# Attention over a recurrent state with a squared-ReLU feed-forward: the state of batches 3 to 7 loaded after the last quarter of w_out, and a list schedule with longer assumed loads

## The chip, the cores and the metric

One Trainium2 chip, one core of it. The metric is device time in microseconds (us), lower is better: the median of the timed executions. One further execution was profiled; all durations in this document come from profiled executions. Engines are named as the profile names them: PE is the matmul engine, PEld its weight loads, DVE, ACT and POOL the three engines that copy, activate and do general work, SP the engine that only issues transfers. A transfer is issued by POOL, SP or ACT and moved by 16 DMA engines that all of them share.

## What is computed

Eight batches, 8 heads, 512 tokens, a state of 32 rows a head, 64 columns; the feed-forward is 512 to 2048 to 512.

```python
def _attn_ref(x, state):                       # x (8,8,512,64), state (8,8,32,64)
    scores = (1/8) * x @ state^T               # softmax over the 32 state rows
    xread = softmax(scores) @ state            # 512 rows a head
    scores2 = (1/8) * state @ x^T              # softmax over the 512 tokens
    sread = softmax(scores2) @ x               # 32 rows a head
    return concat([xread, sread], axis=2)
def _moe_ref(x, w_in, w_out, s, b):            # x: heads side by side, 8*544 rows of 512
    r = maximum(x @ w_in, 0)
    return (s * (r * r) + b) @ w_out
```

## The kernel before

**What is multiplied.** For the 512 token rows of a batch the kernel doesn't form `xread`: it multiplies the state by w_in once per batch (tiles `Mps`, copied to `M`), and multiplies that by the normalised attention weights `a4`, which gives the feed-forward's hidden rows `h` in 16 pieces `f` of 128 rows. `h` is cut at zero by ACT (sometimes DVE) into `g`, squared by DVE, and multiplied by w_out into the two output banks `o_0` and `o_1`. Batch 0 does the last product plainly (`rows_mm`); batches 1 to 7 use a seven-product scheme that needs sums of blocks of `g` (`pd`, DVE) and of w_out (`u`, DVE). The state rows (`V`, `sr`, `srdT`, `h_sr`, `g_sr`) are collected over all batches and go through the feed-forward last.

**Loads.** w_in is loaded in four column pieces `wi_0` to `wi_3`, w_out in four row pieces `wo_0` to `wo_3`, x in a tile `xn_b` a batch; these are issued by POOL (lines 353, 363, 374), which converts to 16 bits on the way, and run one behind the other in its queue. The state comes in three pieces in 32 bits: `stf` for batch 0 (ACT's queue), `stf1` for 1 and 2, `stf2` for 3 to 7 (128 partitions of 640 numbers, 320 KB). `late` (line 381) issues the last two: POOL writes zeros into the tile (line 383), which takes it to POOL's place in the program, and SP issues the transfer behind that (line 384). `stf2` is converted by POOL into `st16` (`cast_st`, line 300), and one transposing transfer on SP (`dma_stT`, line 429) makes `stTd`, the transposed state of batches 3 to 7. `Mps` and the scores `T` of batch 3 are the first to read `stTd`. Batches 3 to 7 also get their transposed x, `xT`, by transposing transfers on SP (line 445), and every batch gets `aT` so (line 604, from `a2`, DVE), which `V` reads. SP issues in program order: `stf2`, the two `aT` pairs of batches 0 and 1, `stTd`, then the four `xT` pieces of batch 3.

**What sets the order.** Every step is handed to `Plan.add` with an engine, an assumed duration, a priority key (lower goes first) and names that it needs and makes. `Plan.order` then plays the program through with these assumed durations and writes each engine's instructions in the order in which it would have started them. On the chip each engine runs its list strictly in that order and waits where something isn't there. Loads have an assumed pace: `("load", span)` lands `span` behind the load before it. `("tp", span)` is for other transfers: they land `span` after issue, or later while loads are still assumed to run. `K` (line 271) holds the constants that the keys are made of.

**The places around the change.** `seq` (line 390) is the list of loads. PE's matmuls all have line 197, through the helper `mm`. A PE step is named below by its output: `h_b_f` is piece f of batch b, `Mps_b_c` is the product with `wi_c`, `wsum_ps` the column sums of w_out for the bias, which need all four `wo`. `Mps_0_3` is the first reader of `wi_3`. Only two buffers hold `h` (pool `psH`), so an `h` starts when ACT or DVE has read the one two before it.

Of the kernel before, what the change touches and what calls it, by code (L numbers as in the profile page):

```python
# [13 lines left out]
class Plan:  # L14
# [6 lines left out]
    def add(self, eng, key, fn, needs=(), makes=(), bufs=(), land=None, tiled=False, after=0.0, spare=0.0):  # L21
        engs = dict([eng]) if isinstance(eng[0], str) else dict(eng)
        for p, b in bufs:
            self.pool_of[b] = p
            self.users[b] = self.users.get(b, 0) + 1
        self.ops.append((engs, key, fn, tuple(needs), tuple(makes), [b for _, b in bufs], land, tiled, after, spare))

    def order(self, filler, fill_until, ready):
# [21 lines left out]
        mode, channel, log, now, done_n = False, 7.0, [], 0.0, 0  # L50
# [17 lines left out]
        while done_n < len(ops):  # L68
            for e in free_at:
                if free_at[e] > now + 1e-9:  # L70
                    continue
                best = None
                look = self.look if e in ("ACT", "DVE") else 0.06
                for i in cand[e]:
                    if since[i] > now + look:
                        continue
                    t = soon(i) - now
                    if t > look:
                        continue
                    k = ops[i][1] + 20.0 * max(0.0, t)  # L80
                    if e == "PE" and ops[i][7] and mode:
                        k -= 4.0
                    if len(ops[i][0]) > 1 and e == "DVE":
                        k += ops[i][9]
                        if free_at["ACT"] <= now + 0.3:
                            continue
                    if best is None or k < best[0]:
                        best = (k, i, t)
                if best is not None and best[2] > 1e-9:
                    continue  # L90
                if best is None:
                    fill = 0.43 if now < 7.0 else 0.22
                    if e == "PE" and now < fill_until and not any(since[i] < now + fill for i in cand[e]):
                        free_at[e] = now + fill
                        times.append(free_at[e])
                        log.append((now, len(log), "PE", filler, "warm", free_at[e]))
                    continue
                i = best[1]
                engs, key, fn, needs, makes, bufs, land, tiled, after, spare = ops[i]
                for x in engs:  # L100
                    cand[x].discard(i)
                for b in bufs:
                    if b not in placed:
                        placed.add(b)
                        allocs[self.pool_of[b]].append(b)
                dur = engs[e]
                if e == "PE":
                    dur += 0.1 * (tiled != mode)
                    mode = tiled
                end = done = now + dur  # L110
                if land is not None:
                    kind, span = land
                    if kind == "load":
                        done = max(channel, end + 2.0) + span
                        channel = max(channel, done)
                    elif now < channel - 4.0:
                        end, done = now + 4.0, now + 9.0
                    else:
                        done = end + span
                free_at[e] = end  # L120
                times.append(end)
                times.append(done + self.hop)
                for m in makes:
                    ready[m] = done + self.hop
                for m in makes:
                    for j in waits.pop(m, ()):
                        count[j] -= 1
# [12 lines left out]
            now = min(nxt) if nxt else now  # L140
# [4 lines left out]
def kernel(  # L145
# [13 lines left out]
    nc = tc.nc  # L159
# [3 lines left out]
    B, H, S, D = x.shape  # L163
# [6 lines left out]
    NG = H // 4  # L170
# [47 lines left out]
    st_v = state.rearrange("b (g hf) j d -> (hf j) (b g) d", g=NG)  # L218
    NB_HW = 3
    stf = konst.tile([P, NG, D], FP32, name="stf")  # L220
    stf1 = konst.tile([P, (NB_HW - 1) * NG, D], FP32, name="stf1")
    stf2 = konst.tile([P, (B - NB_HW) * NG, D], FP32, name="stf2")
# [42 lines left out]
    def late_dma(dst, src):  # L265
# [3 lines left out]
        nc.sync.dma_start(dst, src)  # L269

    K = dict(
        h1=4.0, hs=0.6, M0=-5.6, M1=-0.7, T1=-1.2, x2=24.7, T2=23.1, D2=27.7, M2=23.7, V0=27.1, V1=25.0, u=12.2,
        us=2.0, pd1=12.5, o0=9.0, o2=22.8, w=25.2, r=-0.5, T=-14.5, D=3.1, Mb=5.6, V=12.0, S=3.6, S0=0.1,
        E=-4.5, L=-4.6, a4=-4.7, Mc=4.3, pd=3.5, sp=-0.2,
    )
    A = {b: {"E": {}, "a4": {}} for b in range(B)}
    G, PD, U, SN, OSB = {}, {}, {}, {}, {}
    stTd = konst.tile([P, (B - NB_HW) * NG, P], FP16, name="stTd")
    wi, wo = {}, {}
# [29 lines left out]
    add = plan.add  # L309
# [37 lines left out]
    def load(key, dur, span, fn, makes, bufs=(), after=0.0):  # L347
        add(("POOL", dur), key, fn, [], makes, bufs, ("load", span), after=after)

    def load_wi(c):  # L350
        def fn(e):
            wi[c] = wpool.tile([P, NKM, FC], FP16, name=f"wi_{c}")
            nc.gpsimd.dma_start(  # L353
                out=wi[c],
                in_=moe_w_in.rearrange("(k p) f -> p k f", p=P)[:, :, c * FC : (c + 1) * FC],
            )

        return fn

    def load_wo(q):  # L360
        def fn(e):
            wo[q] = wpool.tile([P, NKF // 4, DM], FP16, name=f"wo_{q}")
            nc.gpsimd.dma_start(  # L363
                out=wo[q],
                in_=moe_w_out.rearrange("(q f p) n -> q p f n", p=P, q=4)[q],
            )

        return fn

    def load_x(b, h0=0, h1=H):  # L370
        def fn(e):
            if h0 == 0:
                xn[b] = xpool.tile([P, H, SCH, D], FP16, name=f"xn_{b}", tag="xn")
            nc.gpsimd.dma_start(  # L374
                out=xn[b][:, h0:h1].rearrange("p h c d -> p h (c d)"),
                in_=x[b, h0:h1].rearrange("h (q c) d -> q h (c d)", q=P),
            )

        return fn

    def late(dst, src):
        def fn(e):
            nc.gpsimd.memset(dst, 0.0)
            nc.sync.dma_start(dst, src)

        return fn
# [1 line left out]
    gate = konst.tile([P, 2], FP16, name="gate")  # L388
    nc.gpsimd.tensor_copy(gate, ident16[:, 0:2])
    seq = [("wi", 0), ("x", 1), ("wi", 1), ("stf1",), ("wo", 0), ("wi", 2), ("wo", 1), ("wi", 3)]  # L390
    seq += [("wo", 2), ("wo", 3), ("x", 2), ("sb",), ("stf2",), ("x", 3), ("x", 4), ("x", 5)]
    for n, it in enumerate(seq):
        key = -40 + n
        if it[0] == "wi":
            load(key, 0.8, 4.2 if it[1] == 0 else 2.65, load_wi(it[1]), [it], after=3.4)
        elif it[0] == "wo":
            load(key, 0.8, 2.65, load_wo(it[1]), [it], after=3.4)
        elif it[0] == "x":
            b = it[1]
            load(  # L400
                key, 0.9, 2.8 if b == 1 else 3.8, load_x(b),
                [("x", b, i) for i in range(4)], [("xn", f"x{b}")], after=3.4,
            )
        elif it[0] == "stf1":
            load(key, 0.3, -3.0, late(stf1, st_v[:, NG : NB_HW * NG, :]), [it], after=3.4)
        elif it[0] == "stf2":
            load(key, 0.6, 1.0, late(stf2, st_v[:, NB_HW * NG :, :]), [it], after=3.4)
        else:
            load(key, 0.15, 0.1, late(s_bc, moe_s.to_broadcast((P, 1))), [("s",)], after=3.4)
            load(key + 0.1, 0.15, 0.1, late(b_bc, moe_b.to_broadcast((P, 1))), [("b",)], after=3.4)  # L410
    n1 = (NB_HW - 1) * NG
    add(
        DV(0.4), 0, lambda e: cast_st(e, stf1, NG, n1),
# [6 lines left out]
    for k in range(8):  # L420
        b, i = 6 + k // 4, k % 4
# [94 lines left out]
    def E_exp(b, g):  # L516
        def fn(e):
# [4 lines left out]
            for m in range(2):  # L522
                nc.scalar.activation(  # L523
                    a["E"][g][:, 256 * m : 256 * m + 256],
                    a["T"][m][:, g, :],
# [609 lines left out]
```

## Time and profile before

| | |
|---|---|
| median of 8 runs | 223.97 us (222.48 to 226.24) |
| the profiled execution's own time | 224.34 us |
| span of its instructions | 222.3 us |
| PE busy | 207.3 us, 93% |
| DVE busy | 164.5 us, 74% |
| ACT busy | 134.6 us, 61% |
| POOL busy | 37.5 us, 17% |
| moved by DMA | 24.04 MB |

The span runs from the first instruction of the program to its last; the profiled execution's time has about 2 us around it. Times inside the span are given as us from its start. In a timeline row stand start, duration, engine, line, operation, output<-input, shape and count; in square brackets the idle time of the engine before it and what ended it. Rows of consecutive instructions of one kind are merged, so a merged row's duration is from the first start to the last end. Matmuls are pipelined: what one costs in a row of equals is best read from the chain, where a row gives the time until the next kind begins. PEclk is the clock that PE was granted, 1.00 at full speed. An issue row gives KB and the us from issue to landing, a median where several are counted.

### The profile page before, as it was taken

Reading aid. Unit: us, or ns where it says so; the run is one execution under the profiler, and the core shown is the slowest. Engines: PE = TensorE matmul, PEld = TensorE weight load, DVE = VectorE, ACT = ScalarE, POOL = GpSimd, SP = SyncE. Lnnn points to the kernel's source line nnn. Section 1 sums busy time; section 2 is a strip of 40 time slices with the busy share of each in tenths; the row PEclk is TensorE's granted clock in tenths of the full one; section 3 lists DMA queues with packets and bytes.
Section 4 is the critical chain, followed back from the end, with each engine's and each line's share of the span. In section 5 each row is a group of like instructions: output and inputs, shape, how many; then the busy total and the mean of one; then the engine's idle time right before and its main releaser. Section 6 shows DMA issues by size and latency. Waiting matters only on the chain.

```text
span 222.3 us, 4924 instructions
## 1 busy us (share of the span) xinstructions
PE 207.3 (93%) x1967; PEld 132.0 (59%) x1967; DVE 164.5 (74%) x390; ACT 134.6 (61%) x293; POOL 37.5 (17%) x60
## 2 busy tenths in 40 slices
PE   5998759999999999999999999999999999999960
PEld 1443213543466767677766676667667777888650
DVE  1379447999898788877997799798889878754330
ACT  4669827779568565974997488559855544332100
POOL 4933111002034152102110101111112102100000
PEclk9999958999999999999999999999999999999997
DMA  6999999997059999902531212122202111210221
GB/s 200 188 200 154 192 201 198 197 172 174 0 134 170 132 167 228 140 10 94 118 99 30 99 47 76 29 97 72 71 18 86 49 47 53 97 47 19 78 80 62
DMA packets 41282, 24.04 MB, mean 108 GB/s; under 512 B 25772, under 2 KB 39340, under 8 KB 41260
## 3 DMA queue, kind: packets, MB, share of 16 engines
q0 software_dynamic: 13840, 15.21, 35.5%
q1 hardware_dynamic: 26860, 8.40, 22.3%
q8 instruction: 15, 0.25, 0.4%
q10 hardware_dynamic: 560, 0.13, 0.3%
q14 instruction: 7, 0.06, 0.1%
HBM read 17.37 MB, written 8.91 MB: 118 GB/s over the span
## 4 chain that ended last, share of the span: by engine, by line
PE 83%; DMA 11%; POOL 2%; DVE 0%; issue 0%
PE o L197 48%; PE h L197 23%; DMA wi<-in_moe_w_in_dram 10%; PE Mps L197 4%; PE h_sr L197 3%; PE V L197 1%; PE D L197 1%; DMA ident<-ident_const 1%; POOL wi L353 1%; PE T L197 1%; POOL wo L363 1%; PE wsum_ps L197 0%; PE bias_ps L197 0%; POOL xn L374 0%; PE xTps L197 0%; DVE osb_last L1075 0%
## 5 line engine op out<-in xcount | busy, mean ns | idle before, releaser
L756 ACT ACTIVATE g<-h 128x512 f16<-128x512 f32 x127 | 74.8, 606 | 50.6 <-PE h L197 48.7
L197 PE MATMUL h<-a,M 128*128 128x512 f16 x256 | 75.3, 385 | 0.3 <-ACT g L756 0.3
L762 DVE TENSOR_TENSOR g<-g 128x512 f16<-128x512 f16 x128 | 52.4, 422 | 6.7 <-ACT g L756 6.6
L197 PEld LDWEIGHTS <-pd 128*128 128x128 f16 x448 | 43.0, 98 | 17.9 <-issue 1.9
L197 PE MATMUL o<-wo,g 128*128 128x256 f16 (+1 forms) x288 | 52.6, 300 | 0.0
L197 PEld LDWEIGHTS <-g 128*128 128x128 f16 x400 | 38.9, 98 | 23.0 <-issue 2.6
L197 PE MATMUL o<-u,pd 128*128 128x256 f16 x336 | 50.5, 273 | 0.0
L998 POOL DMA_DIRECT2D out_dram<-c x24 | 16.3, 678 | 104.6 <-DVE c L990 87.5
L197 PEld LDWEIGHTS <-M 128*128 128x128 f16 x256 | 24.5, 99 | 12.9 <-issue 5.3
L990 DVE SCALAR_TENSOR_TENSOR c<-o,s_bc,bias_bc 128x512 f32<-128x512 f32 x28 | 21.0, 752 | 14.9 <-PE o L197 14.8
L298 ACT CAST M<-Mps 128x512 f16<-128x512 f32 x49 | 27.7, 606 | 1.0 <-PE Mps L197 1.0
L990 DVE SCALAR_TENSOR_TENSOR c<-o,s_bc,c 128x512 f32<-128x512 f32 x21 | 15.8, 750 | 9.0 <-PE o L197 8.8
L197 PE MATMUL o<-u,g 128*128 128x256 f16 x112 | 21.4, 273 | 0.0
L197 PE MATMUL o<-wo,pd 128*128 128x256 f16 x112 | 21.4, 273 | 0.0
L774 DVE TENSOR_TENSOR pd<-g 128x1024 f16<-128x1024 f16 x28 | 19.2, 686 | 0.3
L756 ACT ACTIVATE g_sr<-h_sr 128x256 f16<-128x256 f32 x16 | 6.1, 383 | 12.9 <-PE h_sr L197 12.9
L523 ACT ACTIVATE E<-T 128x256 f16<-128x256 f32 x32 | 11.9, 384 | 1.3 <-PE T L197 1.2
L374 POOL DMA_DIRECT2D xn<-in_x_dram x13 | 10.4, 820 | 10.0 <-DMA wi<-in_moe_w_in_dram 4.7
L785 DVE TENSOR_TENSOR pd<-g,pd 128x512 f16<-128x512 f16 x28 | 11.7, 419 | 0.1
L783 DVE TENSOR_TENSOR pd<-g,pd 128x512 f16<-128x512 f16 x28 | 11.7, 418 | 0.0
L300 DVE CAST M<-Mps 128x512 f16<-128x512 f32 x15 | 10.2, 685 | 0.6 <-PE Mps L197 0.6
L542 ACT ACTIVATE D<-D 128x512 f32<-128x512 f32 x16 | 8.7, 584 | 3.2 <-PE D L197 3.1
(62 smaller groups left out, 156.8 us busy)
## 6 DMA issues: line engine op xcount, KB each, us to landing
out_dram<-c POOLq DMA_DIRECT2D x24, 256.0 KB, 2.5
xn<-in_x_dram POOLq DMA_DIRECT2D x5, 512.0 KB, 24.4
wi<-in_moe_w_in_dram POOLq DMA_DIRECT2D x4, 512.0 KB, 14.0
wo<-in_moe_w_out_dram POOLq DMA_DIRECT2D x4, 512.0 KB, 21.9
xf<-in_x_dram SPq DMA_DIRECT2D x4, 256.0 KB, 3.3
out_dram<-osb POOLq DMA_DIRECT2D x4, 256.0 KB, 3.4
xn<-in_x_dram POOLq DMA_DIRECT2D x8, 128.0 KB, 5.8
out_dram<-c SPq DMA_DIRECT2D x4, 256.0 KB, 2.5
```

Source lines behind the costliest of these rows:

```text
L197: return nc.tensor.matmul(out, lhsT, rhs, start=start, stop=stop, tile_position=tp, is_transpose=is_transpose, skip_group_check=True,)
L298: nc.scalar.copy(dst, src)
L300: ENG[e].tensor_copy(dst, src)
L374: nc.gpsimd.dma_start(out=xn[b][:, h0:h1].rearrange("p h c d -> p h (c d)"), in_=x[b, h0:h1].rearrange("h (q c) d -> q h (c d)", q=P),)
L523: nc.scalar.activation(a["E"][g][:, 256 * m : 256 * m + 256], a["T"][m][:, g, :], AF.Exp, scale=scale, accum_out=a["rs"][:, g, m : m + 1],)
L756: nc.scalar.activation(g_of(name, f), OSB["h", name, f], AF.Relu)
L762: ENG[e].tensor_mul(g_of(name, f), g_of(name, f), g_of(name, f))
L774: nc.vector.tensor_tensor(pd[:, :, 0:2], g4[:, :, 1:2, :].to_broadcast((P, 2, 2, hS)), g4[:, :, 0:4:3, :], ALU.subtract,)
L783: nc.vector.tensor_tensor(pd[:, :, 2], g4[:, :, 3], pd[:, :, 0], ALU.subtract)
L785: nc.vector.tensor_tensor(pd[:, :, 3], g4[:, :, 2], pd[:, :, 2], ALU.subtract)
L990: nc.vector.scalar_tensor_tensor(t, src, s_bc, add, ALU.mult, ALU.add)
L998: ENG[e].dma_start(dst[:, rows:SCH:2, hD * h : hD * h + hD], SN[b, name])
```

## The change

`stf2` leaves the list of loads. It is issued by a step of its own, `load_stf2`: POOL copies two columns of `wo_3` into `stf2`, which can't happen before `wo_3` has landed, and SP issues the transfer behind that. The plan assumes that it lands 4 us after POOL's step (`"side"`, which no longer takes the delay of `"tp"` while loads run). The assumed spans of the loads grow (w_in and w_out 2.65 to 2.8, x 2.8 to 2.9 and 3.8 to 3.9), and 16 of the constants in `K` change, among them M1, T1, V1, D2, V, us. No computation changes, and the instructions are the same but for POOL's zeroing of `stf2`, which becomes the two-column copy, and the engine that runs some casts and cuts.

```diff
-                    elif now < channel - 4.0:
+                    elif kind == "tp" and now < channel - 4.0:
                         end, done = now + 4.0, now + 9.0
                     else:
                         done = end + span
...
-        h1=4.0, hs=0.6, M0=-5.6, M1=-0.7, T1=-1.2, x2=24.7, T2=23.1, D2=27.7, M2=23.7, V0=27.1, V1=25.0, u=12.2,
+        h1=4.3, hs=0.6, M0=-5.6, M1=0.9, T1=0.9, x2=24.4, T2=23.7, D2=25.5, M2=24.1, V0=27.6, V1=20.5, u=12.2,
...
-    seq += [("wo", 2), ("wo", 3), ("x", 2), ("sb",), ("stf2",), ("x", 3), ("x", 4), ("x", 5)]
+    seq += [("wo", 2), ("wo", 3), ("x", 2), ("sb",), ("x", 3), ("x", 4), ("x", 5)]
...
-            load(key, 0.8, 2.65, load_wo(it[1]), [it], after=3.4)
+            load(key, 0.8, 2.8, load_wo(it[1]), [it], after=3.4)
...
-        elif it[0] == "stf2":
-            load(key, 0.6, 1.0, late(stf2, st_v[:, NB_HW * NG :, :]), [it], after=3.4)
...
+    def load_stf2(e):
+        nc.gpsimd.tensor_copy(stf2[:, 0, 0:2], wo[3][:, 0, 0:2])
+        nc.sync.dma_start(stf2, st_v[:, NB_HW * NG :, :])
+
+    add(("POOL", 0.3), -21, load_stf2, [("wo", 3)], [("stf2",)], (), ("side", 4.0))
```

On POOL, behind the load of x for batch 2, stand before:

```order
L374 DMA xn_2_228<-in_x_dram 128x8x256
L383 MEMSET s_bc_114 128x1
L383 MEMSET b_bc_115 128x1
L383 MEMSET stf2_99 128x640
L374 DMA xn_3_262<-in_x_dram 128x8x256
L374 DMA xn_4_268<-in_x_dram 128x8x256
L374 DMA xn_5_287<-in_x_dram 128x8x256
L300 CAST st16_118<-stf2_99 128x10x64 x2
```

and now:

```order
L374 DMA xn_2_228<-in_x_dram 128x8x256
L383 MEMSET s_bc_114 128x1
L383 MEMSET b_bc_115 128x1
L374 DMA xn_3_255<-in_x_dram 128x8x256
L374 DMA xn_4_263<-in_x_dram 128x8x256
L374 DMA xn_5_273<-in_x_dram 128x8x256
L411 CAST stf2_99<-wo_3_217 128x2
L300 CAST st16_118<-stf2_99 128x10x64 x2
```

POOL's step that lets SP issue `stf2` has moved behind all loads up to x of batch 5, and now reads `wo_3`. SP's own list has kept its order.

On PE, from the second matmul of `h_1_4` on, stand before:

```order
L197 MATMUL h_1_4_473<-a4_1_1_413,M_1_325 128x512
L197 LDWEIGHTS stT_0_161
L197 MATMUL Mps_0_3_0_479<-wi_3_195,stT_0_161 32x512
L197 LDWEIGHTS stT_0_161
L197 MATMUL Mps_0_3_1_480<-wi_3_195,stT_0_161 32x512
```

and now the same `Mps_0_3` stands behind two `h`, four matmuls of `o_0` with `wo_1`, and two more `h`, of which these are the last:

```order
L197 MATMUL o_0_121<-wo_1_190,g_0_1_390 128x512
L197 LDWEIGHTS M_1_343
L197 MATMUL h_1_7_496<-a4_1_0_403,M_1_343 128x512
L197 LDWEIGHTS M_1_343
L197 MATMUL h_1_7_496<-a4_1_1_409,M_1_343 128x512
L197 LDWEIGHTS M_0_250
L197 MATMUL h_0_8_501<-a4_0_0_232,M_0_250 128x512
L197 LDWEIGHTS M_0_250
L197 MATMUL h_0_8_501<-a4_0_1_260,M_0_250 128x512
L197 LDWEIGHTS stT_0_161
L197 MATMUL Mps_0_3_0_505<-wi_3_195,stT_0_161 32x512
```

So `h_1_5`, `h_1_6`, `o_0` with `wo_1`, `h_1_7` and `h_0_8`, which stood right behind `Mps_0_3`, now stand right before it. On ACT the cuts of `h_1_5` and `h_1_6` now stand ahead of both casts of `Mps_1_2`, and the cut of `h_0_8` has gone to DVE. What follows on PE up to `wsum_ps` is the same work in nearly the same order. Further on, `T_3` stands about 0.7 us of PE's work earlier (`h_2_7` and three pairs of `o` have moved behind it, one `Mps` of batch 3 ahead of it), and `V` of batches 3 to 7 about 3 us earlier.

More of the change, by code (lines that the diff above doesn't have):

```diff
@@ L271 @@
     K = dict(
-        h1=4.0, hs=0.6, M0=-5.6, M1=-0.7, T1=-1.2, x2=24.7, T2=23.1, D2=27.7, M2=23.7, V0=27.1, V1=25.0, u=12.2,
-        us=2.0, pd1=12.5, o0=9.0, o2=22.8, w=25.2, r=-0.5, T=-14.5, D=3.1, Mb=5.6, V=12.0, S=3.6, S0=0.1,
-        E=-4.5, L=-4.6, a4=-4.7, Mc=4.3, pd=3.5, sp=-0.2,
+        h1=4.3, hs=0.6, M0=-5.6, M1=0.9, T1=0.9, x2=24.4, T2=23.7, D2=25.5, M2=24.1, V0=27.6, V1=20.5, u=12.2,
+        us=5.1, pd1=12.5, o0=9.6, o2=23.0, w=26.2, r=0.7, T=-14.8, D=3.1, Mb=5.5, V=8.6, S=3.6, S0=0.1, E=-4.5,
+        L=-4.6, a4=-4.7, Mc=4.3, pd=3.5, sp=-1.7,
     )
@@ L394 @@
         if it[0] == "wi":
-            load(key, 0.8, 4.2 if it[1] == 0 else 2.65, load_wi(it[1]), [it], after=3.4)
+            load(key, 0.8, 4.2 if it[1] == 0 else 2.8, load_wi(it[1]), [it], after=3.4)
         elif it[0] == "wo":
-            load(key, 0.8, 2.65, load_wo(it[1]), [it], after=3.4)
+            load(key, 0.8, 2.8, load_wo(it[1]), [it], after=3.4)
         elif it[0] == "x":
@@ L400 @@
             load(
-                key, 0.9, 2.8 if b == 1 else 3.8, load_x(b),
+                key, 0.9, 2.9 if b == 1 else 3.9, load_x(b),
                 [("x", b, i) for i in range(4)], [("xn", f"x{b}")], after=3.4,
```

## The prediction, made before the changed kernel was run

> **What bounds the kernel now.** I read PE's waits over the whole span first, then the windows around the longest one, then the chain. The waits:
>
> ```profile
> PE Mps L197 <- DMA wi<-in_moe_w_in_dram: 3.9, 1, 3.9
> ...
> PE Mps L197 <- DVE M L300: 0.4, 1, 0.4
> ```
>
> One wait, 3.9 us for a piece of w_in, is by far the longest; the few others are at the start. PE's timeline places it, and the windows around it give PE's busy time (first figure behind the length), DVE's (third), and behind POOL's count the granted clock, the DMA share and GB/s:
>
> ```profile
> 25.55 1.08 PE L197 MATMUL h<-a,M 128*128 128x512 f16 x4 [0.25 <-ACT g L756]
> 30.49 0.63 PE L197 MATMUL Mps<-wi,stT 64*32 64x512 f16 x8 [3.85 <-DMA wi<-in_moe_w_in_dram]
> ```
>
> ```profile
> 26.60:28.50 1.90, 0.04 (x1) 0.00 (x0) 1.37 (x5) 1.34 (x3) 0.00 (x0) 1.00 1.22 196
> 28.50:30.40 1.90, 0.00 (x0) 0.00 (x0) 1.40 (x5) 0.00 (x0) 0.00 (x0) 0.51 1.22 196
> 35.30:36.30 1.00, 1.00 (x6) 0.52 (x5) 0.14 (x1) 0.77 (x2) 0.00 (x0) 0.96 1.44 196
> 24.80:50.00 25.20, 21.09 (x142) 8.70 (x141) 18.33 (x49) 16.24 (x38) 1.59 (x3) 0.86 1.35 192
> 50.00:215.00 165.00, 164.93 (x1656) 114.52 (x1654) 131.40 (x304) 100.77 (x215) 24.16 (x36) 1.00 0.41 85
> ```
>
> PE stands idle from 26.64 to 30.49, the clock is at half about 1.9 us into that and back at about 35.3, so the first 5 us of work behind the wait run at half speed. From 50 to 215 PE is busy for 164.93 of 165 us. A delay or a gain ahead of that therefore passes to the end unchanged. The chain (start, time until the next piece, what) gives what the slow clock costs:
>
> ```profile
> 30.49 0.63 PE Mps L197 x5
> 31.11 1.82 PE h L197 x4
> 32.94 1.71 PE o L197 x4
> 34.64 1.29 PE h L197 x4
> 35.93 0.86 PE o L197 x4
> 36.80 0.86 PE h L197 x4
> 37.66 0.34 PE Mps L197 x8
> 39.08 0.98 PE wsum_ps L197 x16
> ```
>
> At full clock four `h` or `o` matmuls take 0.86 and an `Mps` 0.34. The first four pieces took 0.63+1.82+1.71+1.29 = 5.45 and would have taken 0.34+3x0.86 = 2.92: 2.53 us lost. The wait and its slow clock thus cost 3.85+2.53 = 6.38 us of the 224.34.
>
> **The change, first part: the order on PE.** `Mps_0_3` no longer stands right behind `h_1_4`; two `h`, four `o`, two `h` come first. Their inputs aside from `wo_1` were there, since PE ran them straight behind `Mps_0_3` before. What paces them is ACT, since `h` has two buffers:
>
> ```profile
> 26.34 1.12 ACT L756 ACTIVATE g<-h 128x512 f16<-128x512 f32 x2
> ```
>
> This row is the cuts of `h_0_7` and `h_1_4`, done at about 26.95 and 27.46. So `h_1_5` starts at 26.95 instead of 26.64 and `h_1_6` at 27.5; from there 0.43+0.86+0.86 brings PE to `Mps_0_3` at 29.65, and through it at 30.0. Before, the same five pieces were done at 35.93. That is 5.93 us gained, 0.45 less than 6.38, if `wo_1` is there at 27.9 and `wi_3` at 29.65. When do they land?
>
> ```profile
> 7.61 0.79 POOL L363 DMA_DIRECT2D wo<-in_moe_w_out_dram  x1
> 8.35 0.80 POOL L353 DMA_DIRECT2D wi<-in_moe_w_in_dram  x1
> 9.08 1.54 POOL L363 DMA_DIRECT2D wo<-in_moe_w_out_dram  x2
> 14.27 0.89 POOL L374 DMA_DIRECT2D xn<-in_x_dram  x1 [3.64 <-DMA xn<-in_x_dram]
> 16.61 0.54 SPq L384 DMA_DIRECT2D stf<-in_state_dram  x1
> ```
>
> ```profile
> wo<-in_moe_w_out_dram POOLq DMA_DIRECT2D x1, 512.0 KB, 19.5
> wi<-in_moe_w_in_dram POOLq DMA_DIRECT2D x1, 512.0 KB, 22.1
> xn<-in_x_dram POOLq DMA_DIRECT2D x1, 512.0 KB, 24.4
> stf<-in_state_dram SPq DMA_DIRECT2D x1, 320.0 KB, 15.7
> DMA to landing us min/median/max: 12.7/21.9/26.1
> ```
>
> Issue plus landing time: `wo_1` 7.61+19.5 = 27.1, `wi_3` 8.35+22.1 = 30.45, `stf2` 32.3, `wo_3` (the longest of the last row, which is that of the `wo`) about 9.85+26.1 = 35.95, x of batch 2 38.7. So even with the old landing `Mps_0_3` would wait 0.8 us, not 3.85: the order does most of the work.
>
> **Second part: `stf2` out of the way.** Its 320 KB ran between about 22 and 32.3, beside `wi_2`, `wo_1`, `wi_3`. From one side the gain is its bytes at the rate of the window, 0.328 MB at 196 GB/s, 1.7 us. From the other: `wo_1` to `wi_3` landed 3.35 us apart, while `wi_3` to `wo_3` took 5.5 for two, and `wo_3` to x of batch 2 2.75; three pieces at some 0.7 too much is 2.1. I take 2.0: `wi_3` lands at 28.45, before PE comes to it, and `wo_3` at 33.95.
>
> That makes `wo_3` the next thing late. `wsum_ps` needs it, and PE, 5.93 us earlier, stands there at 39.08-5.93 = 33.15. It waits 0.85 us, with no effect on the clock at so short a gap (the wait of 0.4 for DVE, at 17, had none). The gain is then 5.93-0.85 = 5.08. x of batch 2 is wanted about 4 us later, at about 38.5, and lands near 37: hidden. POOL's zeroing of `stf2` (0.66 us or less) goes, the two-column copy comes; POOL waits there for nothing that PE needs, and SP has nothing ready to issue behind it before some 36. Both cost nothing.
>
> **Third part: what follows `stf2`.** It is issued at about 34.3 instead of 16.6. Behind it come:
>
> ```profile
> 15.98 0.54 SPq L384 DMA_DIRECT2D b_bc<-in_moe_b_dram  x1
> 32.39 1.57 POOL L300 CAST st<-stf 128x640 f16<-128x640 f32 x2 [7.57 <-DMA stf<-in_state_dram]
> 41.28 5.51 SPq L604 DMA_TRANSPOSE aT<-a  x4
> 46.88 1.28 SPq L429 DMA_TRANSPOSE stTd<-st  x1
> 48.26 5.21 SPq L445 DMA_TRANSPOSE xT<-xn  x4
> ```
>
> ```profile
> stf<-in_state_dram SPq DMA_DIRECT2D x1, 128.0 KB, 7.5
> b_bc<-in_moe_b_dram SPq DMA_DIRECT2D x1, 0.5 KB, 8.1
> aT<-a SPq DMA_TRANSPOSE x16, 3.5
> xT<-xn SPq DMA_TRANSPOSE x2, 3.8
> ```
>
> ```profile
> 55.33 0.42 PE L197 MATMUL V<-xn,aT 128*32 128x64 f16 x32
> 60.01 0.41 PE L197 MATMUL Mps<-wi,stTd 64*32 64x512 f16 x8
> 65.00 0.43 PE L197 MATMUL T<-xT,stTd 64*32 64x256 f16 x16
> ```
>
> The landing is bounded by two rows: 7.5 us (`stf1`, 128 KB beside loads) and the 15.7 that `stf2` took. The second holds a wait behind two tiny transfers of SP, the later of which landed at 15.98+8.1 = 24.1; `stf2` followed 8.2 us later. With some 3 us to get going I take 11: it lands at 45.3, bounds 41.8 and 50.0. Then 1.57 for the cast, 1.28 for `stTd`, 3.9 for three of four `xT` issues and 3.8 to the last landing: `T_3` can start 10.55 us behind the landing, at 55.9. PE comes to it at 65.00-0.7 (order)-5.08 = 59.2. It is hidden by 3.3 us; at the upper bound it waits 1.35. `Mps_3_0` comes at about 60.01-0.4-5.08 = 54.5 and needs `stTd` alone: 1.57 and 1.28 and a landing like that of `xT`, 6.65 behind `stf2`, at 52.0. `V_0`, wanted at 55.33-5.08 = 50.25, needs its `aT`, which are queued behind `stf2`; at the median 3.5 us of an `aT` they land by 48.8. That margin, 1.4, is the thinnest.
>
> The other moves lie in a stretch where PE waited for nothing. DVE has room: from 24.8 to 50 it was busy for 18.33 of 25.2 us, and the stretch gets 5.08 us shorter, which leaves 1.8. `V` of the later batches 3 us earlier finds its `aT` issued some 20 us ahead, as before.
>
> **The sum.** 224.34-3.85-2.53+0.45+0.85 = 219.26 for an execution like the profiled one. That one lay 0.37 over the median of the eight, so 218.9 as a median.
>
> **The rivals.**
> *The loads are not faster.* The DMA engines moved 196 GB/s with `stf2` under way (28.50) and 196 without (35.30). If the pieces of the weights keep a pace of their own, taking 320 KB away changes nothing. Then `wi_3` costs 0.8, PE comes to `wsum_ps` at 33.95, and `wo_3` lands at 35.95: 2.0 us. 6.38-0.45-0.8-2.0 = 3.1 gained, 220.8. If the gap also halves the clock, as 1.9 us did, 2.5 more: 223.4. The 3.35 against 2.75 us between landings speak against it.
> The Trainium skill ("TensorE: Matmul & The Clock Gate", Part 1: The HAM clock gate) has the clock fall after an idle window of about 3.4 us, and its section on HAM oscillation warns of gaps over about that; by that rule a 2.0 us gap would cost no clock and this rival ends at 220.8. The trace disagrees, with 0.51 granted from 28.50.
>
> *`stf2` is late for batch 3 and its queue for `V`.* At the upper bound, 50.0, `aT` lands 3.5 us later, 53.5, and `V_0` waits 3.2 us; `T_3` is then covered. That is 222.1, with a halved clock 224.6, which is no change.
> The Trainium skill ("DMA: Bandwidth & Descriptors", Queues, rings and completion order) says that each DMA engine consumes a queue's descriptors in ring order, so `aT` can't overtake `stf2`; that speaks for this rival, and no row here shows a transpose behind a large load.
>
> *Slower.* The place is `T_3`: its wait and a halved clock must outweigh 5.08+0.67. With 2.53 for the clock the wait must pass 3.2, so `stf2` must land after 59.2+3.2-10.55 = 51.9, 17.6 us from issue, while three loads of x run beside it. At 20 us it is 5.6 and the time 218.9+5.6+2.5 = 227.0. For it: no load of 320 KB was seen faster than 15.7. Against it: SP's queue ahead of it is now empty.
>
> *The order brings nothing*, since DVE, with only 1.8 us to spare, holds `o_0` or the next `h`: waits of 5 us in all take the place of the one removed, 223.9. Against it: where DVE was as full, behind 50 (131.40 of 165 us), PE did not wait.
>
> **How the numbers follow.** Forecast 0.70; loads not faster 0.10 (0.015 of it with the halved clock); late `stf2` 0.13 (0.02 with it); slower 0.05; order brings nothing 0.02. The range reaches from 217.6 (6.38 gained and nothing new: 224.34-6.38-0.37 = 217.6) to 222.1, which takes in the two middle rivals without the clock. 0.3%, 0.67 us, is what a measurement of this kernel can tell. Faster by more: 0.70+0.085+0.11, 0.89 rounded down; within it the two halved clocks and the last rival, 0.06; slower 0.05.
>
> **What would show it.** PE's wait for `wi` gone or under 1 us and the clock 1.00 through 26 to 36; `wsum_ps` waiting about 0.9 for `wo`, PE there 5 us earlier; `wi_3` at about 28.5, x of batch 5 later relative to `wo_3`; no wait at `V` or `T` from 48 to 62; `stf2` landing 11 us after issue. I am wrong if PE shows a wait over 2 us anywhere behind 26, or a halved clock.

## The result and the profile after

| | kernel before | changed kernel |
|---|---|---|
| median | 224.06 us (222.03 to 226.24, 32 runs) | 219.4 us (218.57 to 219.86, 11 runs) |
| profiled execution | 224.34 us | 219.75 us |
| span | 222.3 us | 217.9 us |

The ratio is 0.9798, 95% interval [0.9774, 0.9823]: 4.7 us faster by the medians, where 5.1 had been forecast (218.9 against 223.97). The spread shrank too, from 4.2 us to 1.3. (Ratios here leave out executions of the kernel before that lie over 1.5% above its fastest, so they can stand nearer to 1 than the medians do.)

The page after, first row busy time and instructions of each engine, second the granted clock in 40 slices:

```profile
PE 206.1 (95%) x1967; PEld 132.0 (61%) x1967; DVE 164.6 (76%) x389; ACT 134.5 (62%) x294; POOL 37.7 (17%) x60
...
PEclk9999999999999999999999999999999999999997
```

PE does the same 1967 matmuls in 1.2 us less busy time, and no slice before the last shows a lowered clock any more (before, the sixth and seventh showed 5 and 8 tenths). All of PE's waits of 0.2 us or more:

```profile
PE xTps L197 <- ACT xn L298: 1.4, 2, 1.2
PE o L197 <- DVE warm L212: 1.2, 1, 1.2
PE h L197 <- ACT g L760: 0.6, 2, 0.4
PE stTps L197 <- DVE st L300: 0.5, 1, 0.5
PE Mps L197 <- ACT M L298: 0.3, 1, 0.3
PE Mps L197 <- DVE M L300: 0.2, 1, 0.2
```

None of them is for a transfer. The wait for `wi_3` is gone, and the wait of `wsum_ps` for `wo_3`, which the forecast put in its place, did not come. The timeline of the changed kernel, from the first `stTps` to `wsum_ps` and on to `T_3`:

```profile
16.00 0.28 PE L197 MATMUL stTps<-ident,st 128*128 128x128 f16 x2 [0.52 <-DVE st L300]
...
26.89 1.08 PE L197 MATMUL h<-a,M 128*128 128x512 f16 x4 [0.25 <-ACT g L760]
28.36 1.08 PE L197 MATMUL h<-a,M 128*128 128x512 f16 x4 [0.39 <-ACT g L760]
...
31.10 0.41 PE L197 MATMUL Mps<-wi,stT 64*32 64x512 f16 x8
...
34.69 1.05 PE L197 MATMUL wsum_ps<-wo,ones 128*32 128x512 f16 x16
...
55.45 0.41 PE L197 MATMUL Mps<-wi,stTd 64*32 64x512 f16 x8
60.02 0.40 PE L197 MATMUL T<-xT,stTd 64*32 64x256 f16 x16
```

The row at 26.89 is the one that stood at 25.55 before (both with 0.25 us of idle time ahead): in this execution PE came there 1.34 us later. From it to `Mps_0_3` take 4.21 us, where the forecast had 29.65-25.55 = 4.10. The windows of the changed kernel, read as before (length, then PE, PEld, DVE, ACT, POOL, clock, DMA share, GB/s):

```profile
26.60:28.50 1.90, 1.26 (x6) 0.48 (x5) 1.35 (x4) 1.90 (x5) 0.00 (x0) 1.00 1.25 207
28.50:30.40 1.90, 1.90 (x10) 0.81 (x9) 1.81 (x6) 1.71 (x4) 0.00 (x0) 1.00 1.24 205
24.80:50.00 25.20, 24.56 (x200) 10.17 (x198) 23.26 (x61) 20.73 (x46) 3.43 (x5) 1.00 1.34 196
```

In the two windows in which PE had stood it now works, at full clock, and the loads run at 205 to 207 GB/s instead of 196. From 24.8 to 50 PE is idle for 0.64 us in all: the two waits for ACT. DVE has 1.94 us left there (the forecast had 1.8 for the shorter stretch that holds the same work as before). The chain shows who sets PE's pace now:

```profile
26.28 1.05 ACT g L760 x2
27.33 0.48 ACT M L298
27.80 0.51 ACT g L760
28.36 1.08 PE h L197 x4
...
31.17 0.34 PE Mps L197 x8
...
34.76 0.98 PE wsum_ps L197 x16
```

Up to 28.3 the chain runs through ACT's cuts (`g`) and its cast of `M`, then through PE alone. `wsum_ps` begins at 34.76 instead of 39.08, 4.32 us earlier; the rest of the gain is in what follows it (183.14 us instead of 183.22 to the end of the span) and outside the span (1.85 us instead of 2.04). The issues, from the timeline and the list of transfers:

```profile
8.41 0.80 POOL L353 DMA_DIRECT2D wi<-in_moe_w_in_dram  x1
...
33.23 0.37 SPq L412 DMA_DIRECT2D stf<-in_state_dram  x1
36.77 7.44 SPq L608 DMA_TRANSPOSE aT<-a  x4
```

```profile
wi<-in_moe_w_in_dram POOLq DMA_DIRECT2D x1, 512.0 KB, 19.2
stf<-in_state_dram SPq DMA_DIRECT2D x1, 320.0 KB, 10.5
stTd<-st SPq DMA_TRANSPOSE x1, 7.9
```

`wi_3` landed at 8.41+19.2 = 27.6 (before 30.45), `stf2` at 43.7, 10.5 us after issue.

### The profile page after: what moved, and what is told of

The parts are those of the page before. It is cut to its first block, busy times and chain, and to the rows that moved or that the text cites. A ratio compares the mean times of both kernels' runs of the same rounds, so it can differ in the third digit from the quotient of the medians.

```text
span 217.9 us, 4922 instructions
## 1 busy us (share of the span) xinstructions
PE 206.1 (95%) x1967; PEld 132.0 (61%) x1967; DVE 164.6 (76%) x389; ACT 134.5 (62%) x294; POOL 37.7 (17%) x60
## 4 chain that ended last, share of the span: by engine, by line
PE 86%; DMA 5%; ACT 3%; POOL 1%; DVE 0%; issue 0%
PE o L197 50%; PE h L197 24%; DMA stf<-in_state_dram 4%; PE Mps L197 4%; PE h_sr L197 3%; ACT g L760 2%; PE D L197 2%; PE V L197 1%; DMA ident<-ident_const 1%; PE T L197 1%; POOL wi L353 1%; ACT M L298 1%; PE xTps L197 1%; ACT E L527 1%; PE wsum_ps L197 0%; POOL xn L374 0%
## 5 line engine op out<-in xcount | busy, mean ns | idle before, releaser
L760 ACT ACTIVATE g<-h 128x512 f16<-128x512 f32 x125 | 73.4, 605 | 43.6 <-PE h L197 41.6
L197 PE MATMUL h<-a,M 128*128 128x512 f16 x256 | 73.7, 379 | 0.6 <-ACT g L760 0.6
L197 PE MATMUL o<-u,pd 128*128 128x256 f16 x336 | 51.8, 273 | 0.0
L197 PE MATMUL o<-wo,g 128*128 128x256 f16 (+1 forms) x288 | 51.6, 296 | 0.0
L298 ACT CAST M<-Mps 128x512 f16<-128x512 f32 x52 | 29.5, 611 | 4.0 <-PE Mps L197 4.0
L778 DVE TENSOR_TENSOR pd<-g 128x1024 f16<-128x1024 f16 x28 | 19.2, 685 | 0.2
L197 PE MATMUL o<-warm 128*128 128x512 f16 x23 | 8.5, 498 | 1.2 <-DVE warm L212 1.2
## 6 DMA issues: line engine op xcount, KB each, us to landing
wo<-in_moe_w_out_dram POOLq DMA_DIRECT2D x4, 512.0 KB, 19.2
```

Of the source, the lines that this page charges most:

```text
L197: return nc.tensor.matmul(out, lhsT, rhs, start=start, stop=stop, tile_position=tp, is_transpose=is_transpose, skip_group_check=True,)
L298: nc.scalar.copy(dst, src)
L760: nc.scalar.activation(g_of(name, f), OSB["h", name, f], AF.Relu)
L778: nc.vector.tensor_tensor(pd[:, :, 0:2], g4[:, :, 1:2, :].to_broadcast((P, 2, 2, hS)), g4[:, :, 0:4:3, :], ALU.subtract,)
```

## The experiments

Every kernel was timed beside the kernel before on the same chip, in three sets of four. The medians of the kernel before were 222.48 (e1 to e4), 222.06 (e5 to e8) and 222.82 us (e9 to e12), lower than the 224.06 of the comparison above, from which the expectations start; what was measured is compared within a set.

| kernel | median, us | ratio to before, 95% interval |
|---|---|---|
| e1 new order alone | 219.09 (218.68 to 219.79) | 0.9861 [0.982, 0.9902] |
| e2 new place of `stf2` alone | 219.44 (218.84 to 220.52) | 0.9869 [0.9825, 0.9912] |
| e3 before, PE kept busy in the wait | 222.51 (222.02 to 223.11) | 1.0012 [0.9985, 1.0038] |
| e4 changed, `stf2` not held for `wo_3` | 219.49 (218.74 to 220.78) | 0.9881 [0.9835, 0.9927] |
| e5 changed, `stf2` held for x of batch 5 | 219.61 (218.53 to 219.88) | 0.9881 [0.9824, 0.9937] |
| e6 before, unchanged | 222.42 (220.39 to 225.03) | 0.9989 [0.9945, 1.0034] |
| e7 before, `Mps_0_3` alone moved | 221.37 (220.54 to 222.09) | 0.9991 [0.9956, 1.0027] |
| e8 changed, unchanged | 218.57 (217.87 to 219.47) | 0.984 [0.9785, 0.9894] |
| e9 before, half of the wait kept busy | 222.03 (221.05 to 223.27) | 0.9974 [0.9943, 1.0005] |
| e10 e7 with two sets of sums moved | 221.19 (220.01 to 222.58) | 0.9943 [0.9912, 0.9974] |
| e11 changed, one cast on DVE | 219.05 (218.33 to 219.95) | 0.985 [0.9805, 0.9894] |
| e12 changed, unchanged | 218.92 (218.47 to 220.41) | 0.9855 [0.9804, 0.9906] |

My theory is the forecast's: the gain is the wait for `wi_3` and the half clock behind it. The rivals that the runs were to tell apart from it: only one of the two halves of the change matters; the half clock is no cost in the median; and the queue behind `stf2` or a full DVE gives part of it back.

**e1: the new order with the old place of `stf2`.** The step is moved in the finished list; the rest is the changed kernel.

```diff
...
+    st = next(t for t in steps if t[4] == (("stf2",),))
+    steps.remove(st)
+    at = next(n for n, t in enumerate(steps) if ("b",) in list(t[4]))
+    steps.insert(at + 1, st[:3] + (late(stf2, st_v[:, NB_HW * NG :, :]),) + st[4:])
```

> The changed kernel's order on every engine, with stf2 back in its old place: zeroed by POOL and issued by SP behind the two scalars, ahead of x of batch 3, so that it runs beside the weights. My theory (the order takes most of the stall away, the place gives the loads about 2 us): wi_3 lands at about 30.4 as in the kernel before, PE comes to Mps_0_3 at about 31 and does not wait, wo_3 lands near 36 and wsum_ps, wanted at 34.8, waits about 1.2 us; clock 1.00 all the way; 220.6 us. Rival (the place of stf2 makes the gain, the order only follows): PE still waits several us for wi_3 and the time is 223.5 or more.

Measured 219.09, no wait for any transfer. From e1's chain, and the answer for its four `wi`, of which `wi_3`, issued at 7.88, took longest:

```profile
33.73 0.98 PE wsum_ps L197 x16
```

```profile
DMA to landing us min/median/max: 7.1/13.4/20.8
```

The order with `stf2` in its old place brings nearly the whole gain, 3.4 us. The time is 1.5 us below the expected one, by as much as the kernel before was lower in this set, but the wait of 1.2 us for `wo_3` didn't come: the loads were early, `wi_3` at 7.9+20.8 = 28.7 and `wo_3` at 10.2+23.6 = 33.8, though `stf2` was in its old place. In the profiles with the old order and place `wo_3` landed at 35.5 to 36.0, and the last matmuls of `wsum_ps`, which need it, began at 34.3 in e1. So up to 1.6 us of e1's gain may be due to these early loads, which the last section comes back to, and not to the order by itself.

**e2: the new place with the old order**, with `load_stf2` as in the change.

```diff
...
+    at = next(n for n, t in enumerate(steps) if ("x", 5, 0) in list(t[4]))
+    steps.insert(at + 1, st[:3] + (load_stf2,) + st[4:])
```

> The order of the kernel before on every engine, only stf2 issued behind wo_3 as in the change. My theory: wi_3 lands about 2.4 us earlier, near 28.0, PE still waits for it at Mps_0_3 but 1.4 us instead of 3.85; whether a gap of 1.4 us halves the clock decides between 219.2 (no) and 221.6 (yes), and I expect 221, between the two, with some executions of either kind. Rival (place alone makes the whole gain): 219.4 with no wait for wi_3 left.

The timeline of e2, and its windows:

```profile
28.99 0.41 PE L197 MATMUL Mps<-wi,stT 64*32 64x512 f16 x8 [1.62 <-DMA wi<-in_moe_w_in_dram]
```

```profile
27.00:29.00 2.00, 0.38 (x5) 0.01 (x4) 2.00 (x7) 1.67 (x4) 0.00 (x0) 1.00 1.24 205
29.00:31.00 2.00, 2.00 (x16) 0.90 (x17) 0.62 (x2) 1.02 (x3) 0.00 (x0) 1.00 1.26 206
31.00:33.00 2.00, 2.00 (x11) 0.88 (x9) 1.94 (x6) 1.84 (x5) 0.00 (x0) 1.00 1.42 198
```

A wait of 1.62 us stays, its end 1.5 us earlier than before (30.49), and the clock is not lowered behind it. The median is 219.44, near the 219.2 expected for a full clock; the profiled execution is the slowest of the six (220.52), so a usual one may have waited less. Each half by itself brings about as much as both (3.4 and 3.0 us, against 3.5 and 3.9 for both in the other sets), since both halves shorten the same wait. What the first half leaves, the second covers.

**e3: PE kept busy through the wait.** The kernel before with 16 matmuls by zeros ahead of the sums of `Mps_0_3`, into the same tile; they add nothing to the result.

```diff
+            if (b, c) == (0, 3):
+                for _ in range(16):
+                    mm(ps[0], warm[:, 0:P], warm)
```

> The kernel before, with 16 extra matmuls of zeros on PE ahead of Mps_0_3, written into Mps_0_3's own tile, which the real matmuls then overwrite. They fill 3.4 us of the 3.85 us wait for wi_3. My theory (the idle wait halves the clock, which costs 2.5 us behind it): the clock stays 1.00, the h and o behind the wait take 0.86 us for four, the time falls by 2.5 us to 221.5. Rival (matmuls behind the wait are slow since the transfers hold their operands, or the clock falls by itself): they stay slow and the time stays within 0.5 us of 224.0.

Measured 222.51, as the kernel before, with a spread of 1.1 us instead of 3.75. In e3's timeline the zeros fill PE until after `wi_3` has landed (8.2+22.2 = 30.4):

```profile
27.32 3.61 PE L197 MATMUL Mps<-warm 128*128 128x512 f16 x16
30.87 0.41 PE L197 MATMUL Mps<-wi,stT 64*32 64x512 f16 x8
```

The zeros fix the lost time at 3.55 us from start to start, whatever the load does, and the clock stays at 1.00. From e3 to e1 is 222.51-219.09 = 3.42 us. 0.4 of it is the zeros' own, since they run past the landing, so the wait net of ACT's pacing is about 3.0, for which the forecast had 3.85-0.45 = 3.40. That e3 gained nothing in the median says that the half clock cost less than 2.53 us in most executions, or that the zeros (0.4 us past the landing) ate part of it; e6 and e9 were to tell.

**e6: the kernel before once more.**

> The kernel before, unchanged, for the spread of its executions and the mean clock of its profile. My theory (the wait for wi_3 halves the clock for a stretch that depends on when the wait falls in the clock's own period, so the 2.5 us read from one profile are near the upper end, and the typical cost is about half): executions spread over 3 us or more, from 221 with the clock hardly halved to 224.5; a profile with a short halved stretch has a short span. Rival (2.5 us are lost each time, and chips differ): executions within 1 us of each other, as those of the changed kernel are.

Its chain behind the wait, and two windows, of which the last four fields are the POOL count, clock, DMA share and GB/s:

```profile
30.52 0.41 PE Mps L197 x8
30.93 1.18 PE h L197 x4
32.11 1.71 PE o L197 x4
33.81 1.50 PE h L197 x4
```

```profile
28.00:30.00 2.00, 0.00 (x0) 0.00 (x0) 1.92 (x6) 0.04 (x1) 0.00 (x0) 1.00 1.22 196
32.00:34.00 2.00, 2.00 (x6) 0.66 (x5) 1.87 (x4) 1.17 (x3) 0.64 (x1) 0.50 1.32 201
```

The wait is the same, 3.8 us, but the clock is still full throughout it and falls only behind it. The first four pieces lose 0.41+1.18+1.71+1.50-2.92 = 1.88 us instead of 2.53. The twelve executions of e6 differ likewise: the four with a mean clock of 0.991 to 0.993 took 220.4 to 221.4 us, the six with 0.984 to 0.988 took 222.2 to 223.8, the two with 0.980 took 224.9 and 225.0. The loss by the clock is a matter of the execution.

**e9: only half of the wait kept busy.** As e3, with 8 matmuls (`range(8)`), which end before `wi_3` lands.

> The kernel before with 8 matmuls by zeros (8 x 0.21 = 1.7 us) ahead of the sums of Mps_0_3, into the same tile, so that PE's idle time for wi_3 shrinks from 3.8 us to about 2 us while the time at which wi_3 lands stays. If the halved clock behind the wait is a cost that comes and goes with the length of the idle time: the clock stays near 1.00 in all executions, the median falls by 1.0 to 1.3 us to about 221.0 and the spread narrows from over 4 us to about 2. If the clock costs nothing in the median: 222.3, as the kernel before.

```profile
27.13 1.89 PE L197 MATMUL Mps<-warm 128*128 128x512 f16 x8
30.51 0.41 PE L197 MATMUL Mps<-wi,stT 64*32 64x512 f16 x8 [1.49 <-DMA wi<-in_moe_w_in_dram]
```

`Mps_0_3` begins at 30.51 as in e6 (30.52), so the load's part is the same, and the clock is another: 0.990 to 0.995 in all twelve executions, where the kernel before ranged from 0.980 to 0.994. The median is 222.03, 0.8 us below the kernel before; by the interval the gain is between none and 0.57%, 1.3 us. That lies between the two expectations (221.0 and 222.3), so by this run the cost of the clock in the median is about 0.8 us, between none and 1.3; in the two profiled executions it was 1.9 and 2.5. It didn't need PE to be busy throughout: cutting the idle time from 3.8 us to 1.5 was enough. From e9, with the old wait and a full clock, to the changed kernel in the same set (e12) is 222.03-218.92 = 3.1 us, which is the wait net of ACT's pacing once more.

**e4 and e5: what `stf2` waits for.** e4 issues it at its new place without waiting for `wo_3`; e5 holds it until x of batch 5 has landed.

```diff
-        nc.gpsimd.tensor_copy(stf2[:, 0, 0:2], wo[3][:, 0, 0:2])
+        nc.gpsimd.memset(stf2, 0.0)
```

and for e5

```diff
-        nc.gpsimd.tensor_copy(stf2[:, 0, 0:2], wo[3][:, 0, 0:2])
+        nc.gpsimd.tensor_copy(stf2[:, 0, 0:2], xn[5][:, 0, 0, 0:2])
```

> The changed kernel, but stf2 does not wait for wo_3: POOL zeroes it at the same place in its list, behind the issue of x of batch 5 at about 23.8, and SP issues it then. It runs beside wi_3, wo_2, wo_3 and x of batch 2. My theory: wi_3 loses under 1 us and is still there before PE, wo_3 lands at about 34.5 and wsum_ps waits 0 to 0.3 us; no change to the changed kernel, 219.3 to 219.8. Rival (the wait for wo_3 is what brings the gain): 220.5 or more, with a wait for a weight of over 1 us.

> The changed kernel, but POOL's step that lets stf2 go copies two columns of x of batch 5 instead of wo_3, so that stf2 is issued some 13 us later, at about 46, and the aT transposes that SP issues behind it go out after 46.5 instead of 36.8. My theory (V_0 and T_3 are hidden by some us only, V_0 least): V_0, wanted at about 51, waits 1 to 2 us for aT, T_3, wanted at about 60, waits 0 to 1.5; 221 to 222 us, no halved clock. Rival (what follows stf2 has room to spare of 10 us or more): no wait, 219.4.

e4, 219.49, is as the changed kernel and as expected: issued at 25.2, `stf2` came too late to hold up `wi_3`, which landed at 8.0+20.6 = 28.6, 2.5 us before PE came to it. In e5, 219.61 (1.0 us above e8 on the same chip by the medians, 0.2 by the spans), the place that the forecast called the thinnest shows. The timelines of SP and of PE in e5, and its list of transfers:

```profile
44.57 0.38 SPq L412 DMA_DIRECT2D stf<-in_state_dram  x1
45.05 6.33 SPq L608 DMA_TRANSPOSE aT<-a  x4
51.47 1.28 SPq L433 DMA_TRANSPOSE stTd<-st  x1
```

```profile
54.90 0.42 PE L197 MATMUL V<-xn,aT 128*32 128x64 f16 x32 [0.52 <-DMA aT<-a]
```

```profile
stf<-in_state_dram SPq DMA_DIRECT2D x1, 320.0 KB, 3.3
```

`V_1` waits 0.5 us for its `aT`, which stood behind `stf2` in SP's queue; `V_0` and `T_3` wait for nothing. The time expected, 221 to 222, didn't come, because `stf2` without loads beside it landed in 3.3 us: issued 11.3 us later than in the changed kernel, it landed 47.9-43.7 = 4.2 later.

**e7: only `Mps_0_3` moved**, behind `h_0_8`, in the kernel before.

```diff
...
+    st = next(t for t in steps if ("Mps", 0, 3) in list(t[4]))
+    steps.remove(st)
+    at = next(n for n, t in enumerate(steps) if ("h", 0, 8) in list(t[4]))
+    steps.insert(at + 1, st)
```

> The kernel before with one step moved on PE: the eight matmuls of Mps_0_3 stand behind h_1_5, h_1_6, o_0 with wo_1, h_1_7 and h_0_8 as in the changed kernel, all else as before, stf2 among the weights. My theory (that place is what the order gains): no wait for wi_3 over 1 us, clock 1.00, ratio to the kernel before within 0.005 of that of the changed kernel, about 219.5. Rival (the new order as a whole, or the loads, are needed): more than 1 us above the changed kernel of the same session.

Measured 221.37, 0.7 below the kernel before (no change by the ratio), 2.8 above e8: the expectation failed. The wait for `wi` is gone and the clock is full. The timelines of DVE and of PE in e7:

```profile
31.96 0.42 DVE L833 TENSOR_TENSOR u<-wo 128x512 f16<-128x512 f16 x1 [1.84 <-DMA wo<-in_moe_w_out_dram]
```

```profile
37.08 0.39 PE L197 MATMUL o<-wo,g 128*128 128x512 f16 x1 [0.32 <-DVE g L762]
39.73 1.12 PE L197 MATMUL bias_ps<-wsum,ones 128*128 128x512 f32 x2 [0.51 <-DVE wsum L300]
```

DVE stands for `wo_2` with a sum of `u_2`, with squares queued behind it, and is then late for PE twice, by 0.83 us together. That is the rival in which a full DVE holds PE; the changed kernel, whose list moves DVE's work along with PE's, has neither wait. The two explain 0.8 of the 2.8 us to e8: e7's profiled execution (220.62) lies 0.75 below its median and e8's (219.47) 0.9 above, and the rest isn't shown.

**e10: e7 with those sums moved too**, the four of `u_2` behind the square of `h_0_9`, the four of `u_3` behind the copy of `bias_out` (`behind` takes a step out of the list and puts it behind another).

```diff
...
+    behind(("Mps", 0, 3), ("h", 0, 8))
+    for n in (3, 2, 1, 0):
+        behind(("u", 2, n), ("g", 0, 9))
+        behind(("u", 3, n), "bias")
```

> The kernel before with Mps_0_3 moved behind h_0_8, as in the run of one move, and on VectorE the sums of u_2 moved behind the square of h_0_9 and those of u_3 behind the copy of bias_out. If VectorE's standing for wo_2 was what kept the one move from paying: no wait of PE for VectorE at o_1_0 or bias_ps, and a time at least 1 us below that of the one move, 220.0 or less, near the changed kernel. If the rest of the new order matters besides: it stays near 221.4.

Measured 221.19. By the ratio that is 0.6% faster than the kernel before, which e7 was not, but still 2.3 us above e12 on the same chip, where 220.0 or less had been expected if the sums were all that was wrong. The waits at `o` and `bias_ps` went, as expected. In e10's timeline of PE stands what replaced them:

```profile
42.89 0.43 PE L197 MATMUL T<-xT,stT 64*32 64x256 f16 x15 [0.66 <-DVE xT L300]
```

The four sums of `u_3` now run on DVE from 39.55 to 41.02 ahead of the copies of `stT` and `xT`, and `T` waits 0.66 us for these. That is one place. e10's profiled execution was its fastest (220.01, 1.5 us above that of e12); the rest of its distance from e12 in the medians isn't shown by a profile and stays open.

**e11 and e12: is ACT's chain the next bound?** In the changed kernel, the first cast of `Mps_0_2` on DVE; e12 is the changed kernel itself on the same chip.

```diff
-        step[3](step[2])
+        step[3]("DVE" if ("M", 0, 2, 0) in list(step[4]) else step[2])
```

> The changed kernel with the cast of the first half of Mps_0_2 on VectorE instead of ScalarE. If ScalarE's chain of squares and casts from 24.7 to 28.3 us now sets when PE gets h_1_5 and h_1_6: 0.3 to 0.5 us faster than the changed kernel. If VectorE, busy 1.3 of 1.9 us there, can't take it in time: no change, within 0.2 us.

> The changed kernel as it is, beside the three others on the same chip: 218.6 to 219.6 by all theories.

219.05 and 218.92: no gain. PE's wait at the second `h` fell from 0.39 to 0.20 us, and the first stayed at 0.25: too little for these runs to see. e8, the changed kernel in the second set, had this expectation:

> The changed kernel, unchanged, to stand beside the others on one chip. My theory (the two halves cover the same stall, so that both together bring little over either): within 0.5 us of e1 and e2, 219.0 to 219.5. Rival (the halves add): 1 us or more below them, under 218.3.

It gave 218.57, between the two, and its profiled execution had no wait for a transfer.

## Why the prediction was right, and where its sizes were off

- **The wait for `wi_3`, 3.85 less 0.45 for ACT's pacing: right, at most a little large.** e9 against e12 gives 3.1 us and e3 against e1 about 3.0, for 3.40; the way from the first `h` that waits for ACT to `Mps_0_3` is 4.21 us for 4.10.
- **The half clock, 2.53: the mechanism right, the size too large for a median.** It was read from one execution. From `Mps_0_3` to `wsum_ps` that one took 39.08-30.49 = 8.59 us, e6 38.46-30.52 = 7.94, and e9, at full clock, 36.76-30.51 = 6.25: over this way the clock cost 2.34 and 1.69, 0.19 less than the first four pieces show. The record of the granted clock has one low stretch behind the wait, 6.83 us long in the kernel before (28.55 to 35.38) and 3.41 in e6 (31.56 to 34.97). The mean clocks of the kernel before fall into three groups: of 74 executions (e6's and those timed beside e1 to e12), 24 had 0.989 to 0.994 and a median of 221.1 us, 43 had 0.984 to 0.988 (e6's profile: 0.987) and 222.9, 7 had 0.979 or 0.980 (the first profile: 0.979) and 224.6. So most lost about what e6 did. The first group may also have waited less, so 1.7 us between the groups is an upper reading; e9 gives 0.8. With 3.1 for the wait the gain is 3.9 to 4.8 us. The medians gave 4.7 in the first comparison, 222.06-218.57 = 3.5 and 222.82-218.92 = 3.9 later.
- **The new wait for `wo_3`, 0.85: did not come**, in none of the profiles of the changed kernel or of e1. `wo_3`, the last of `wo`, landed at about 10.30+22.3 = 32.6, where 33.95 had been reckoned, and PE came at 34.69. The term was also too large by its own numbers: `wsum_ps` goes through `wo_0` to `wo_3` in turn, and only its last four matmuls, 0.66 us behind the first, read `wo_3`. PE, there at 33.15, would have wanted it at 33.8 and waited 0.1. e7 shows it: `wsum_ps` began at 34.09 and ran through, though `wo_3` landed at 9.86+24.6 = 34.5. Beside this error stands one of about its size in the other direction:
- **Not in the sum: PE's own start.** PE was 1.34 us later at the first `h` that waits for ACT (26.89 for 25.55). 1.13 us was there at the first `h` of all (14.01 for 12.88), the wait of 0.52 for `stf1` came on top (9.1 us to land instead of 7.5), and some was won back. The first part is the clock at the start of the program. The same matmuls by zeros in the kernel before and in the changed one:

```profile
8.39 0.59 PE L197 MATMUL o<-warm 128*128 128x512 f16 x2
```

```profile
8.72 1.06 PE L197 MATMUL o<-warm 128*128 128x512 f16 x2
```

The record of the granted clock has its first full stretch from 8.07 us on before and from 10.40 on here (the windows show 1.00 ahead of its first entry too). Over the profiles it began at 7.5 to 9.2 us in the seven with the old order on PE (e7 and e10 among them) and at 7.8 to 11.9 in the seven with the new one; whether the order has a part in that isn't shown. e12, where it began at 8.76, came to the same row at 25.66 and to `Mps_0_3` at 29.86, where the forecast had 29.65, so the change can do without this loss. It counts now as it did not before: in all three profiles with the old wait (before, e6, e9) `Mps_0_3` began at 30.49 to 30.52, however early PE was there, while the changed kernel gets there 4.2 us after this row, at whatever time that is. For the profiled execution: +1.34+0.11 and 0.16 in later pieces, less 0.85, less 0.08 behind `wsum_ps` and 0.19 outside the span, is +0.49: 219.26 became 219.75. The nearness of the total is partly luck: these two errors lie in opposite directions.
- **"The order does most of the work": not so.** e2 shows the place alone to do as much. The forecast counted what the order saves and gave the place the rest; tried apart, either is nearly enough.
- **`stf2`'s load, 11 us: 10.5**; and **`V` and `T_3` hidden: right**, with more room than reckoned (e5). `stTd` was the term too small: 7.9 us to land where 3.8 was taken from a row of `xT`. It landed at 45.68+7.9 = 53.6, and `Mps_3_0` came at 55.45: 1.9 us to spare.
- **The rivals.** That loads would not get faster: 207 against 196 GB/s in the same window speaks against it, and e2's wait ended 1.5 us earlier. The queue behind `stf2`: real, but 0.5 us even when issued 11 us later (e5). In the changed kernel one `aT`, issued at 36.8 while `stf2` was still loading, took 9.5 us to land, against a median of 2.7 for all; but without `stf2` ahead of it the first `aT` took 6.3 us in the kernel before and 7.1 and 7.2 in e1 and e4, so `stf2` accounts for 2 to 3 us. The answer for `aT` in the window from 36 to 46 us:

```profile
DMA to landing us min/median/max: 9.5/9.5/9.5
```

The Trainium skill ("DMA: Bandwidth & Descriptors", Queues, rings and completion order) has each DMA engine take a queue's descriptors in ring order, and this row agrees: this `aT` landed at 46.3, 2.6 us behind `stf2`. The same passage lets a later descriptor finish its write first, which the forecast's "can't overtake" leaves out; in none of the five profiles with such an `aT` (after, e2, e8, e11, e12) did it. *DVE holds PE*: shown real for a partial move, 0.8 us in e7 and 0.7 in e10, and avoided by the whole list.
- **The gap that doesn't halve the clock.** The rival's 2.0 us gap was priced with and without the half clock. e2 (1.62 us, clock full) speaks for without; a gap of 2.0 was not run. The Trainium skill ("TensorE: Matmul & The Clock Gate", Part 1: The HAM clock gate) counts activity in a free-running window of about 3.4 us and calls the number of slow matmuls at a kernel's start run-variable. The runs agree: the low stretches lasted 3.41 us and twice that, one idle time of 3.8 us halved the clock 1.9 us into it in one execution and 1.0 us behind its end in another, and no gap of 1.62 us or less did.

## What to carry to other kernels

When an engine stands for a load, price the wait and the slow clock behind it apart: the load ended the wait at the same time within 0.1 us in the profiles with the old order and place, while the clock's loss differed from execution to execution, so take it from many times with their mean clocks and not from one profile. Once the load no longer sets the time, the engine's own arrival does, so take that from more than one profile too. Two remedies for one wait don't add: measure each alone before giving the gain to either. And where one instruction is moved past a late load, move the work of the other engines that was placed around it too: a single move (e7) took the wait of 3.8 us away, put two waits for a full DVE in its place, 0.83 us together, and left the median as it was within the noise.

## What the runs showed that was not expected

- The transfer of `stf2` took more from the weights than its bytes. In the packet records of the kernel before, from 24 to 30 us, each 2 us carry 309 to 311 KB of weights in some 310 packets of mostly 1 KB, and 79 to 81 KB of `stf2` in some 310 packets of 256 B: one for one. In the changed kernel the weights get 409 to 411 KB in the same time.
- From 20 to 22 us the loads were slowed in most profiles: 72 to 138 GB/s in nine of the fourteen, 161 to 201 in five. The window in the kernel before, and in e5:

```profile
20.00:22.00 2.00, 2.00 (x12) 0.88 (x10) 2.00 (x5) 2.00 (x6) 0.01 (x1) 1.00 0.56 72
```

```profile
20.00:22.00 2.00, 2.00 (x17) 0.78 (x17) 1.54 (x5) 2.00 (x5) 0.88 (x1) 1.00 1.38 201
```

72 GB/s against 201. In that stretch the two tiny loads `s_bc` and `b_bc` run, 128 rows of one number each, as 4-byte packets. Yet e5 has them too, at the same time, and no dip, so they alone don't explain it. No run was made for it.
- `wi_3` landed at 30.4 to 30.5 in all four profiles with the old order and the old place (before, e3, e6, e9), but at 28.1 to 29.1 in the three with `Mps_0_3` moved and `stf2` in its old place (e1, e7, e10), which is as early as with `stf2` out of the way (27.5 to 28.9). Why a change of order on PE goes with earlier landings is open. It isn't the bytes moved by then: up to 28 us the queue of the loads had moved 3.81 MB in e9 (landing at 30.5), 3.82 in e10 (28.1) and 3.72 in e7 (29.1). In e1, e7 and e10 `stf2` was issued at 15.9 to 16.1 instead of 16.5 to 17.4.
